# A gated mix of memory attention and a SwiGLU layer on one core: moving value blocks, remainders and two x tables, and ending the seventh Strassen product in the fifth one's bank

## The chip, the core and the metric

The kernel runs on one core of one Trainium2 chip. The metric is the device time of one execution in microseconds (us). Five engines work side by side, each through its own list of instructions in order: PE (TensorE: matmuls; the loads of its weights are the separate row PEld), DVE (VectorE), ACT (ScalarE), POOL (GpSimd) and SP, which here only issues transfers. Matmuls write into eight PSUM banks; a bank is called bank0 to bank7 below.

## The reference

For 2048 rows `x` of width 576, an attention branch `a` and a feed-forward branch `b` are mixed by a gate per row. The attention has 32 heads of width 18 and works in four segments of 512 rows: softmax inside a segment, and a running memory `M`, `z` from the segments before it.

```
for s in range(4):                       # segments of 512 rows
    p = softmax(qs @ ks.T * scale + mask)
    a_dot = p @ vs
    a_mem = (phi(qs) @ M) / (phi(qs) @ z + 1e-6)
    outs.append(g * a_mem + (1 - g) * a_dot)
    M += phi(ks).T @ vs;  z += sum(phi(ks))
a = concat(outs) @ wo
b = (silu(x @ w_gate) * (x @ w_up)) @ w_down      # inner width 4608
out = sigmoid(x . gate_w) * a + (1 - sigmoid(x . gate_w)) * b
```

## The kernel before, in words

**Numbers.** Every fp32 operand is split into a rounded high part, made by ACT, and a low part (the remainder, value minus high part), made by DVE with a `tensor_sub`. A product is then high times high, high times low and low times high: three matmuls instead of one.

**First stage (0 to some 221 us).** Per segment, nine chains of 14 matmuls give q and k (`qk`), eight steps give the values (`v_step`, lines 383 to 404), and from the second segment on each such step is followed by one memory bank (`mem_step`, lines 449 to 469): five or six small matmuls on `Mm` and `phi`, then four DVE operations. A step n takes rows n//2, bank n%2.

**Second stage (to some 1632 us).** Two halves of the rows (`half` 0 and 1), each with 36 tiles of the inner width: 72 *positions*. A position computes gate and up product of one tile, 2x2 in blocks, by a Strassen form with seven products P0 to P6. `seven(t, j)` issues product j: six 128x512 matmuls (line 1018, weights from a tile `wo_`, x from a slot `xo`) and one for the last 64 rows (line 1021). The results chain through PSUM: P0 goes to bank0 (`a`), ACT copies it to bank1 (`xx`), P2 and P4 add to `a`, P3 adds to `xx`. There are two sums on DVE: `y = a + p5` after P2 (line 1087, called the *y add* here) and `p5 = a + p5` after P4 (line 1095, the *p5 add*). After P4, ACT copies `a` into bank1 once more (line 1094), P6 adds to that copy, and DVE multiplies it with the silu (line 1103).

Between products stands a `tick()`, eight in a position, k = 0 to 7, k = 0 behind P0, 1 behind P1, 2 behind the y add, 3 behind P3, 4 behind the p5 add, 5 and 6 behind P5, 7 behind P6. A tick runs `beat`, which first calls what was deferred to it and then adds attention and down products:

- *Deferred work* is the next position's weights: sums of raw tiles on POOL (`total`), high parts on ACT (`high`), remainders on DVE (`low`, line 271). The tables `HIGH` and `LOW` give the tick of each; product 4's remainder comes at k = 1 and product 6's at k = 3 of the position that uses it. The results `hh`, `hl` of a position are split two ticks later in the same way (`split_by`, line 963), the first remainder of them at k = 1.
- *Down products* (`down_group`, line 868): nine matmuls into one of bank3, 4 and 7 and one DVE add into `ya` (line 878). Sixteen of them come in every third position (f % 3 == 0, f > 0), called a *position with groups* here, two or three in a tick from k = 2.
- *Attention steps* (`att_gen`). A unit has six steps; steps 0 to 4 each put a set of logits in a bank (`s_bank`, bf16 matmuls of line 726, row maxima on DVE, line 732); one step later ACT makes the exponentials (`e_bank`, line 744), three steps later DVE rounds them (`p_bank`, line 758) and POOL subtracts (line 759), then a transfer transposes them. A finished unit becomes a *value block* (`v_unit`): 40 small matmuls (lines 774 and 775) and a DVE reduction (line 781). While groups are pending, it is issued at step 5, otherwise at the next unit's step 0, just ahead of that step's logits.

`ts_tile` picks the bank for logits and value blocks: the longest unused of 5 and 6 while groups are pending, else of 5, 6, 7, 3, 4; the first request after groups were fed may get bank7 (`fed`).

At the change of halves ten beats without products (`BREAK`) hold the last sixteen groups. There the second half's x is loaded, summed by POOL and split into new slots (`x_second`, by the tables `LOADS`, `SUMS` and `PARTS`: beat, x half, product). Beat numbers 8 to 17 of these tables lie in the break, 18 to 25 are ticks 0 to 7 of the second half's first position.

When attention has ended, `c_open` frees its memory and loads the output weights `wo` in six pieces into tiles named `raw` (`wo_load`, line 910), which ACT and DVE split five and seven beats later. The **last stage** (from some 1632 us) transposes attention results and multiplies them with `wo`, mixed with the last down products.

Order on each engine is the order in which this program is written out; waits are added where tiles or banks are shared.

Of the kernel before, what the change touches and what calls it, by code (L numbers as in the profile page):

```python
# [20 lines left out]
P = 128  # L21
S = 2048
D = 576
# [25 lines left out]
SHARE = (0, 0, 2, 2, 3, 3, 3, 3)  # L49
BREAK = 10  # L50
LOADS = ((-3, 0, 0), (-2, 0, 1), (3, 1, 0), (4, 1, 3), (4, 0, 3), (5, 0, 2), (5, 1, 1), (6, 1, 2))
SUMS = ((2, 0, 1), (9, 0, 4), (10, 0, 2), (10, 1, 1), (11, 1, 4), (12, 0, 6), (12, 1, 2), (13, 1, 6))
PARTS = ((1, 0, 0), (4, 0, 1), (10, 1, 0), (10, 0, 5), (11, 0, 3), (11, 1, 5), (12, 1, 3), (13, 0, 4), (14, 0, 2),
         (14, 1, 1), (15, 1, 4), (16, 1, 2), (17, 0, 6), (18, 1, 6))
FIRST = (9, 10, 11, 15, 17, 17, 19)
SLOT = (0, 3, 2, 1, 4, 6, 5)
RPOS = (0, 1, 4, 2, 5, 6, 3)
# [9 lines left out]
def gated_mix(ctx, tc, xT, xrest, wf, wfr, wfh, wd, wv, wo, beta, cmask, ident, bmask, out):  # L67
# [39 lines left out]
    first_tile = banks(0, 1, 2, 3, 4)  # L107
    lone_tile = banks(7)
    v_tile = banks(5, 6, 7, 4, 0, 5, 6, 7, *8 * (5, 6, 7))
    a_tile = banks(0)  # L110
    x_tile = banks(1)
    y_tile = banks(2)
    taken = {}
    clock = [0]
# [7 lines left out]

    def ts_tile(shape=(P, L)):
        ids = (5, 6) if groups else (5, 6, 7, 3, 4)
        if fed and groups[0][0] < FT // CH - 1 and max(taken, key=taken.get) != 7:
            ids = (7,)
        fed.clear()
        return ps.tile(list(shape), F32, name=f"bank{soonest(ids, HELD)}")

    def group_tile(shape=(P, L)):  # L130
        return ps.tile(list(shape), F32, name=f"bank{soonest((3, 4, 7), 1)}")

    groups = []

    def split(hi, lo, src):
        nc.scalar.activation(hi, src, AF.Copy)
# [119 lines left out]
    def w_make(half, f, LOW=LOW):  # L256
        g, u = wraw_of.pop(f)
        ops = wops[half, f] = [None] * 7
        a11, a12, a21, a22 = g[:, 0:2], g[:, 2:4], u[:, 0:2], u[:, 2:4]
        src = [a11, None, None, a12, None, None, a22]  # L260

        def total(j, p, q, sub=True):
            src[j] = rp.tile([P, 2, P], F32, name="ws", bufs=3)
            (nc.gpsimd.tensor_sub if sub else nc.gpsimd.tensor_add)(src[j], p(), q())  # L264

        def high(j):
            ops[j] = op_tile()
            nc.scalar.activation(ops[j][:, 0], src[j], AF.Copy)

        def low(j):  # L270
            nc.vector.tensor_sub(ops[j][:, 1], src[j], f32(ops[j][:, 0]))  # L271

        def keep(j):
            nc.sync.dma_start(wc[f, j], f32(ops[j]).rearrange("p a k n -> p (a k n)"))

        todo = [(LEAD - 2, lambda: total(1, lambda: a21, lambda: a22, False)),
                (LEAD - 1, lambda: total(2, lambda: src[1], lambda: a11)),
                (LEAD + 2, lambda: total(4, lambda: a11, lambda: a21)),
                (LEAD + 4, lambda: total(5, lambda: a12, lambda: src[2]))]
        for j in range(7):  # L280
            todo += [(HIGH[j], lambda j=j: high(j)), (LOW[j], lambda j=j: low(j))]
            if half == 0 and f < KEPT:
                todo.append((LEAD + j + 3, lambda j=j: keep(j)))
        return sorted(todo, key=lambda t: t[0])
# [3 lines left out]
    with ExitStack() as st:  # L288
# [310 lines left out]
        for s in range(NSEG):  # L599
# [58 lines left out]
            for n in range(8):  # L658
                hf, i = divmod(n, 4)
                flush()  # L660
                v_step(s, hf, i)
                if s:
                    mem_step(s, n // 2, n % 2)
                if s < 3:
                    if n == 0:
                        xs_of[s + 1] = x_tiles(s + 1)
                    if 1 <= n < 6:
                        x_split(xs_of[s + 1], n - 1, raws["x", n - 1])
                else:
                    if n == 4:  # L670
                        wraw_of[1] = [w_load(1, u) for u in range(2)]
                    if n < 2:
                        first_sum(6, n)
                    elif n < 6:
                        if n < 4:
                            nc.gpsimd.memset(f32(rhs[n - 2][96:]), 0.0)
                        if 3 <= n < 5:
                            r_fetch(n - 3)
                    if n > 2:
                        for z in stack_loads(0)[2 * n - 6:2 * n - 4]:  # L680
                            nc.sync.dma_start(*z)
                    for _ in range((0, 0, 2, 3, 3, 3, 3, 3)[n]):
                        if start[0][0] < 8:
                            start.pop(0)[1]()
# [5 lines left out]
    with ExitStack() as st:  # L690
# [107 lines left out]
        def att_gen():  # L798
# [6 lines left out]
            for tau in range(N + 10):  # L805
# [13 lines left out]
                    e_bank(z)  # L819
                if n == 5 and 1 <= u <= 2 * NB:  # L820
                    held.append(u)
                if held and (groups or n == 0):
                    v = held.pop()
                    v_unit(v - 1)
                    if v % 4 == 1 and v // 4 + 1 < 4 * NSEG:
                        v_fetch(v // 4 + 1)
# [73 lines left out]
        def gates():  # L900
            nc.vector.tensor_scalar_add(gg, gg, 1.0)
            nc.vector.reciprocal(gg, gg)
            nc.vector.tensor_scalar(g1, gg, -1.0, 1.0, op0=OP.mult, op1=OP.add)

        def wo_load(n, hf, c):
            box = []

            def load():
                box.append(raw_tile()[:, :96 * NT].rearrange("p (k n) -> p k n", n=96))
                nc.sync.dma_start(box[0], wo[:, :, 288 * hf + c.start:288 * hf + c.stop])  # L910

            defer(n, load)
            defer(n + 5, lambda: nc.scalar.activation(wos[hf][:, 0, :, c], box[0], AF.Copy))
            defer(n + 7, lambda: nc.vector.tensor_sub(wos[hf][:, 1, :, c], box[0], f32(wos[hf][:, 0, :, c])))
# [45 lines left out]

        def split_by(k, hi, lo, src):
            defer(k, lambda: nc.scalar.activation(hi, src, AF.Copy))  # L962
            defer(k + 1, lambda: nc.vector.tensor_sub(lo, src, f32(hi)))  # L963

        def beat(k=None, half=0):
            for fn in due.popleft() if due else ():
# [62 lines left out]
        for pos, (half, f) in enumerate(seq):  # L1029
# [27 lines left out]
            def tick():  # L1057
# [4 lines left out]
                if half == 0:  # L1062
                    if (q, k) in ((0, 3), (1, 3), (2, 2)):
                        draw[f] = d_load(f)
                    if (q, k) in ((1, 1), (1, 7), (2, 4)):
                        g = f - 1 if k == 1 else f
                        ds[half, g] = d_split(g, draw.pop(g))
                elif (q, k) in ((1, 0), (1, 2), (2, 1)):
                    g = f - 1 if k == 0 else f
                    ds[half, g] = d_fetch(g)  # L1070
                beat(k, half)

            ops, rem = wops.pop((half, f)), rhs[f % 2]
            hh = fp.tile([P, 2, L], F32R, name="hh")
            hl = fp.tile([P, 2, L], F32R, name="hl")
            hs[half, f] = hh, hl
            a, y, xx = a_tile(), y_tile(), x_tile()
            p5, sg0, sg1 = (row_tile() for _ in range(3))
            seven(a, 0)
            nc.scalar.activation(xx, a, AF.Copy)  # L1080
# [4 lines left out]
            seven(a, 2, False)  # L1085
            y = y_tile()
            nc.vector.tensor_add(y, a, p5)
            tick()
            seven(xx, 3, False)
            nc.scalar.activation(sg0, xx, AF.Copy)  # L1090
            tick()
            seven(a, 4, False)
            xx = x_tile()
            nc.scalar.activation(xx, a, AF.Copy)  # L1094
            nc.vector.tensor_add(p5, a, p5)  # L1095
            tick()
            nc.scalar.activation(sg0, sg0, AF.Silu)  # L1097
            seven(y, 5, False)
            nc.scalar.activation(sg1, y, AF.Silu)
            tick()  # L1100
            tick()
            seven(xx, 6, False)
            nc.vector.tensor_mul(sg0, xx, sg0)
            nc.vector.tensor_mul(sg1, p5, sg1)
            if q == CH - 1:
                defer(2, lambda t=(hh[:, 0], hl[:, 0], sg0): split(*t))
# [112 lines left out]
```

## Time and profile before

| what | value |
|---|---|
| median of 3 runs | 1724.15 us (1723.75 to 1724.97) |
| profiled execution: its time, and its span | 1724.43 us, 1722.7 us |
| PE busy | 1706.5 us (99%) |
| weight loads (PEld) busy | 1481.0 us (86%) |
| DVE busy | 1359.8 us (79%) |
| ACT busy | 1084.8 us (63%) |
| POOL busy | 938.4 us (54%) |
| DMA queue q1, share of 16 engines | 77.5% |

The profile is of one execution; times in the timeline are us from the span's start. A row of the timeline has start, length, engine, line, operation, operands, how many were merged, and in brackets the idle time ahead of it with what ended it. Matmuls are pipelined and their ends modelled, so a short stall of PE is counted as busy: the distance between starts tells more than the idle time does.

### The profile page before, as it was taken

What the parts mean: (1) busy time and instruction counts of PE and PEld (TensorE: products, weight loads), DVE (VectorE), ACT (ScalarE), POOL (GpSimd) and SP (SyncE); (2) the same over time, 40 slices, a digit from 0 to 9 for tenths busy, and PEclk for the clock granted to TensorE, in tenths of its full rate; (3) what the DMA queues carried; (4) which work ended last, traced back from release to release, by engine and by line L of the source; (5) the groups of instructions that cost most, each with busy time, mean ns of one, the idle gap of its engine ahead of it and who ended that gap; (6) DMA issues with size and microseconds to landing.
All of it is one profiled execution on the core that took longest, in us unless ns stands there. A gap on an engine that the chain in (4) does not pass through costs nothing.

```text
span 1722.7 us, 34832 instructions
## 1 busy us (share of the span) xinstructions
PE 1706.5 (99%) x11868; PEld 1481.0 (86%) x11868; DVE 1359.8 (79%) x3231; ACT 1084.8 (63%) x2123; POOL 938.4 (54%) x1194
## 2 busy tenths in 40 slices
PE   9999999999999999999999999999999999999999
PEld 7899978888888888888887888888888888888899
DVE  6557588898899889898989677788887778778655
ACT  7666585776677577667765755765666576566411
POOL 4434646666666656565666555555555555555221
PEclk9999999999999999999999999999999999999999
DMA  8654499999998898988879986887778677767544
GB/s 284 233 186 153 151 311 191 232 226 186 209 227 192 181 215 200 193 198 203 210 144 256 290 177 133 178 186 162 148 181 182 147 157 185 163 132 167 165 144 137
DMA packets 524002, 328.05 MB, mean 190 GB/s; under 512 B 411184, under 2 KB 460336, under 8 KB 523824
## 3 DMA queue, kind: packets, MB, share of 16 engines
q1 hardware_dynamic: 523824, 325.83, 77.5%
q8 instruction: 93, 1.52, 0.4%
q14 instruction: 85, 0.70, 0.1%
HBM read 165.76 MB, written 76.09 MB: 140 GB/s over the span
## 4 chain that ended last, share of the span: by engine, by line
PE 83%; DVE 6%; ACT 5%; DMA 3%; issue 2%; POOL 1%; SPq 1%; DVEq 0%; ACTq 0%; POOLq 0%
PE bank L1018 33%; PE bank L868 24%; PE bank L159 10%; PE bank L1021 5%; PE bank L726 4%; PE bank L774 2%; PE bank L775 1%; PE bank L414 1%; ACT pe L744 1%; ACT L744 1%; PE bank L460 1%; DVE xo L137 1%; DVE p L758 1%; DVE scr L732 1%; PE bank L350 1%
## 5 line engine op out<-in xcount | busy, mean ns | idle before, releaser
L759 POOL TENSOR_TENSOR p<-pe,p 128x512 f16<-128x512 f32 x320 | 376.0, 1175 | 420.4 <-DVE p L758 406.2
L868 PE MATMUL bank<-dw,hh 128*128 128x320 f32 (+1 forms) x2304 | 489.0, 305 | 2.8 <-DVE ya L878 2.8
L868 PEld LDWEIGHTS bank<-dw,hh 128*128 128x128 f32 x2304 | 381.4, 190 | 14.4 <-DVE ya L878 3.8
L744 ACT ACTIVATE pe<-bank,mb 128x512 f32<-128x512 f32 (+3 forms) x512 | 247.9, 526 | 197.7 <-DVE mb L732 191.3
L868 PE MATMUL bank<-dw,hl 128*128 128x320 f32 (+1 forms) x1152 | 340.6, 296 | 0.2 <-DVE hl L137 0.2
L732 DVE CUSTOM_DVE_ANT_0 scr<-bank,cm 128x512 bf16<-128x512 f32 (+3 forms) x512 | 246.6, 482 | 6.8 <-PE bank L726 0.2
L878 DVE TENSOR_TENSOR ya<-bank,ya 128x320 f32<-128x320 f32 x352 | 158.3, 453 | 83.9 <-PE bank L868 83.2
L868 PEld LDWEIGHTS bank<-dw,hl 128*128 128x128 f32 x1152 | 218.0, 189 | 0.4 <-DVE hl L137 0.4
L1021 PE MATMUL bank<-xr,rh 128*128 128x512 f32 x504 | 196.5, 390 | 0.0
L752 POOL TENSOR_SCALAR_AFFINE_SELECT pe<-pe 128x256 f32<-128x256 f32 (+1 forms) x320 | 149.8, 469 | 54.1 <-ACT pe L744 51.0
L758 DVE CAST p<-pe 128x512 f16<-128x512 f32 x320 | 152.5, 477 | 0.0
L264 POOL TENSOR_TENSOR ws<-raw 128x256 f32<-128x256 f32 x140 | 118.3, 845 | 17.4 <-DMA raw<-in_wf_dram 4.5
L726 PE MATMUL bank<-kst,qst 108*128 108x512 bf16 (+3 forms) x512 | 125.2, 306 | 2.1 <-ACT pe L744 2.1
L1021 PEld LDWEIGHTS bank<-xr,rh 128*128 128x128 f32 x504 | 94.7, 188 | 20.3
L963 DVE TENSOR_TENSOR hl<-row,hh 128x512 fp32r<-128x512 f32 x120 | 104.2, 868 | 8.3 <-ACT hh L962 7.8
L1095 DVE TENSOR_TENSOR row<-bank,row 128x512 f32<-128x512 f32 x72 | 49.7, 690 | 64.7 <-ACT bank L1094 64.5
L744 ACT ACT_TABLE_LOAD x69 | 88.5, 1283 | 11.1 <-DVE mb L732 10.1
L1080 ACT ACTIVATE bank<-bank 128x512 f32<-128x512 f32 x72 | 41.9, 582 | 80.5 <-PE bank L1021 77.4
L1090 ACT ACTIVATE row<-bank 128x512 f32<-128x512 f32 x72 | 43.3, 601 | 78.0 <-PE bank L1021 77.8
L1097 ACT ACT_TABLE_LOAD x71 | 91.1, 1283 | 1.3
L264 POOL TENSOR_TENSOR ws<-raw,ws 128x256 f32<-128x256 f32 x70 | 58.3, 833 | 49.4 <-DVE wo__22504 L271 10.9
L159 PE MATMUL bank<-xo,qhi 128*128 128x512 f32 x264 | 83.2, 396 | 0.4 <-ACT vps L399 0.4
(2166 smaller groups left out, 4097.9 us busy)
## 6 DMA issues: line engine op xcount, KB each, us to landing
raw<-in_wf_dram SPq DMA_DIRECT2D x140, 256.0 KB
rh<-rc SPq DMA_DIRECT2D x72, 336.0 KB
dc<-dw SPq DMA_DIRECT2D x36, 576.0 KB
dw<-dc SPq DMA_DIRECT2D x36, 576.0 KB
stk<-q SPq DMA_DIRECT2D x32, 384.0 KB
draw<-in_wd_dram SPq DMA_DIRECT2D x36, 288.0 KB
rc<-rt SPq DMA_DIRECT2D x42, 224.0 KB
vd<-vps SPq DMA_DIRECT2D x8, 912.0 KB
```

Of the source, the lines that this page charges most:

```text
L159: nc.tensor.matmul(t, st[n], mv[n], start=(n == 0), stop=(n == 13))
L264: (nc.gpsimd.tensor_sub if sub else nc.gpsimd.tensor_add)(src[j], p(), q())
L726: nc.tensor.matmul(t[:, c:c + w], qs[:KR, pr, P * i:P * i + P], ks[:KR, pr, 0:w], start=True, stop=True)
L732: nc.vector.tensor_tensor_reduce(scr[:, :w], t[:, c:c + w], cm[:, L - w:L], -SCALE, 3.0e38, OP.add, OP.min, m[:, k:k + 1])
L744: nc.scalar.activation(pe[:, c:c + w], t[:, c:c + w], AF.Exp, bias=m[:, k:k + 1], scale=SCALE)
L752: nc.gpsimd.affine_select(d, d, pattern=pat, compare_op=OP.is_ge, fill=0.0, base=0, channel_multiplier=1)
L758: nc.vector.tensor_copy(p[:, 0], pe)
L759: nc.gpsimd.tensor_sub(p[:, 1], pe, p[:, 0])
L868: nc.tensor.matmul(ts[m], p, q[:, cs], start=(n == 0), stop=(n == 3 * CH - 1))
L878: nc.vector.tensor_add(ya[:, i, cs], t, ya[:, i, cs])
L1018: nc.tensor.matmul(t, w[:, p, z], x[z][:, q], start=first and n == 0, stop=False, skip_group_check=True)
L1021: nc.tensor.matmul(t, rem[:, RPOS[j]], XR[j], start=False, stop=True, skip_group_check=True)
```

## The change

Seven edits:

1. **Seventh product.** `a` and `xx` take their banks in turn from 0, 1, 1, 0. P6 adds onto `a` itself, ACT's copy of line 1094 is gone, and the multiplication reads `a`.
2. **Remainders behind the two sums.** In ticks 1 and 3 the remainders made by `low` and `split_by` are put aside (`behind`) and issued after the y add or the p5 add (`let_go`).
3. **Values with logits.** A value block is always issued at step 0, ahead of that step's logits; only logits use up the mark `fed`.
4. **Memory banks in pairs.** In the first stage both memory banks of a row tile follow the odd step.
5. **x's parts.** `SUMS` and `PARTS` get other beats: four parts of the first x half move to beats 17 to 22, most of the second half's come a beat or two earlier.
6. **Output weights.** Pieces 3 and 4 are loaded into new tiles `wr`, the fifth into the tile `draw`, instead of `raw`.
7. Nothing else is computed or left out; sums and products are the same.

```diff
-SUMS = ((2, 0, 1), (9, 0, 4), (10, 0, 2), (10, 1, 1), (11, 1, 4), (12, 0, 6), (12, 1, 2), (13, 1, 6))
-PARTS = ((1, 0, 0), (4, 0, 1), (10, 1, 0), (10, 0, 5), (11, 0, 3), (11, 1, 5), (12, 1, 3), (13, 0, 4), (14, 0, 2),
-         (14, 1, 1), (15, 1, 4), (16, 1, 2), (17, 0, 6), (18, 1, 6))
+SUMS = ((2, 0, 1), (9, 0, 4), (10, 1, 1), (11, 1, 4), (12, 1, 2), (13, 1, 6), (14, 0, 2), (19, 0, 6))
+PARTS = ((1, 0, 0), (4, 0, 1), (10, 1, 0), (11, 1, 5), (12, 1, 3), (13, 0, 5), (13, 1, 1), (14, 1, 4), (15, 1, 2),
+         (17, 0, 2), (17, 1, 6), (18, 0, 3), (20, 0, 4), (22, 0, 6))
...
-    a_tile = banks(0)
-    x_tile = banks(1)
+    ax_tile = banks(0, 1, 1, 0)
...
-        if fed and groups[0][0] < FT // CH - 1 and max(taken, key=taken.get) != 7:
-            ids = (7,)
-        fed.clear()
+        if fed and len(shape) == 2:
+            if groups[0][0] < FT // CH - 1 and max(taken, key=taken.get) != 7:
+                ids = (7,)
+            fed.clear()
...
+    stash, holds = [], [False]
+
+    def behind(fn):
+        if holds[0]:
+            stash.append(fn)
+        else:
+            fn()
+
+    def let_go():
+        while stash:
+            stash.pop(0)()
...
         def low(j):
-            nc.vector.tensor_sub(ops[j][:, 1], src[j], f32(ops[j][:, 0]))
+            behind(lambda: nc.vector.tensor_sub(ops[j][:, 1], src[j], f32(ops[j][:, 0])))
...
-                if s:
-                    mem_step(s, n // 2, n % 2)
+                if s and n % 2:
+                    for bank in range(2):
+                        mem_step(s, n // 2, bank)
...
-                if held and (groups or n == 0):
+                if held and n == 0:
...
+        def wo_home(n):
+            if n in (4, 5):
+                return cps[0].tile([P, 96 * NT], F32, name="wr", bufs=2)
+            if n == 8:
+                return fp.tile([P, D], F32, name="draw", bufs=1)[:, :96 * NT]
+            return raw_tile()[:, :96 * NT]
...
-                box.append(raw_tile()[:, :96 * NT].rearrange("p (k n) -> p k n", n=96))
+                box.append(wo_home(n).rearrange("p (k n) -> p k n", n=96))
...
-            defer(k + 1, lambda: nc.vector.tensor_sub(lo, src, f32(hi)))
+            defer(k + 1, lambda: behind(lambda: nc.vector.tensor_sub(lo, src, f32(hi))))
...
+                holds[0] = k in (1, 3)
                 beat(k, half)
+                holds[0] = False
...
-            a, y, xx = a_tile(), y_tile(), x_tile()
+            a, y, xx = ax_tile(), y_tile(), ax_tile()
...
             nc.vector.tensor_add(y, a, p5)
+            let_go()
             tick()
...
             seven(a, 4, False)
-            xx = x_tile()
-            nc.scalar.activation(xx, a, AF.Copy)
             nc.vector.tensor_add(p5, a, p5)
+            let_go()
             tick()
...
-            seven(xx, 6, False)
-            nc.vector.tensor_mul(sg0, xx, sg0)
+            seven(a, 6, False)
+            nc.vector.tensor_mul(sg0, a, sg0)
```

Two places show what moved. In the changed kernel's rows the same code has other line numbers: 786 and 738 for value blocks and logits, 880 for down products, 1037 for products, 282 and 982 for remainders, 1108 and 1115 for the two sums.

The first is on PE, in position 9 (the first half's tile 9, with groups), from P0 on. Of each run of matmuls into one bank the first row stands here; the bank is the number after `bank`. Before:

```order
L774 MATMUL bank7_4889<-v_3341,pt_4439 128x57
...
L726 MATMUL bank5_4931<-kst1_2324,qst1_2323 128x512
...
L868 MATMUL bank4_4988<-dw_4585,hh_3999 128x320 x2
...
L726 MATMUL bank5_5010<-kst1_2324,qst1_2323 128x128
...
L868 MATMUL bank4_5136<-dw_4585,hh_3999 128x320 x2
...
L774 MATMUL bank6_5154<-v_3341,pt_4771 128x57
...
L1018 MATMUL bank2_4974<-xo60_1736,wo__4880 128x512 x3
...
L726 MATMUL bank5_5228<-kst0_2322,qst0_2321 128x512
```

And after the change:

```order
L786 MATMUL bank5_4871<-v_3360,pt_4425 128x57
...
L738 MATMUL bank7_4913<-kst1_2324,qst1_2323 128x512
...
L880 MATMUL bank4_4970<-dw_4571,hh_3987 128x320 x2
...
L738 MATMUL bank5_4992<-kst1_2324,qst1_2323 128x128
...
L1037 MATMUL bank2_4955<-xo60_1726,wo__4862 128x512 x3
...
L786 MATMUL bank6_5165<-v_3360,pt_4753 128x57
...
L738 MATMUL bank5_5208<-kst0_2322,qst0_2321 128x512
```

The first value block and its logits have changed banks, so that the third set of logits now takes the value block's bank and not that of the first set. The second value block, which stood alone between a down product and P5, now stands right ahead of logits. Counted over the whole list, a value block stands right ahead of logits 62 times of 64 instead of 25 times.

The second place is on DVE, in position 19, from the tick behind P1 to the p5 add. Before:

```order
L271 TENSOR_TENSOR wo__8088<-ws_7941,wo__8088 128x256
L963 TENSOR_TENSOR hl_7602<-row_7607,hh_7601 128x512
L758 CAST p_8186<-pe_8104 128x512
L781 TENSOR_REDUCE acc_8230<-bank3_8189 128x152
L732 ISA scr_8236,mb0_2325<-bank5_8234,cm_84 128x512
L732 ISA mb0_2325 128x1
L1087 TENSOR_TENSOR bank2_8247<-bank0_8150,row_8153 128x512
L271 TENSOR_TENSOR wo__8165<-ws_8083,wo__8165 128x256
L963 TENSOR_TENSOR hl_7602<-row_7608,hh_7601 128x512
L963 TENSOR_TENSOR dw_8176<-draw_7773,dw_8176 128x576
L271 TENSOR_TENSOR wo__8178<-raw_7579,wo__8178 128x256
```

After, in the same stretch:

```order
L770 CAST p_8146<-pe_8066 128x512
L793 TENSOR_REDUCE acc_8190<-bank3_8149 128x152
L744 ISA scr_8196,mb0_2325<-bank5_8194,cm_84 128x512
L744 ISA mb0_2325 128x1
L1108 TENSOR_TENSOR bank2_8207<-bank1_8112,row_8115 128x512
L282 TENSOR_TENSOR wo__8050<-ws_7861,wo__8050 128x256
L982 TENSOR_TENSOR hl_7566<-row_7571,hh_7565 128x512
L282 TENSOR_TENSOR wo__8127<-ws_8045,wo__8127 128x256
L982 TENSOR_TENSOR hl_7566<-row_7572,hh_7565 128x512
L982 TENSOR_TENSOR dw_8138<-draw_7737,dw_8138 128x576
L770 CAST p_8237<-pe_8104 128x512
```

The first two rows of before (product 4's remainder and a remainder of the position before) now stand behind the y add; the last row of before (product 6's remainder) has gone behind the p5 add.

## The prediction

> **What bounds the kernel now.** I read the page first, then PE's waits, then the busy time in stretches, then the timeline where a wait or an edit lies. From the page:
>
> ```profile
> span 1722.7 us, 34832 instructions
> PE 1706.5 (99%) x11868; PEld 1481.0 (86%) x11868; DVE 1359.8 (79%) x3231; ACT 1084.8 (63%) x2123; POOL 938.4 (54%) x1194
> ```
>
> PE is the bound: only 16.2 us of the span are not booked as busy. So an edit pays only where it shortens PE's own list or ends one of PE's waits, and ACT's relief alone pays nothing. The waits on PE and on its weight loads, with us in total, times, longest:
>
> ```profile
> PE bank L1018 <- ACT bank L1094: 3.6, 6, 1.4
> PE bank L868 <- DVE ya L878: 2.8, 4, 0.9
> PE bank L726 <- ACT pe L744: 2.1, 6, 0.4
> PE bank L1018 <- DVE bank L1087: 1.1, 2, 0.7
> PEld bank L1018 <- ACT bank L1094: 8.0, 11, 1.9
> PEld bank L1018 <- DVE bank L1087: 3.5, 7, 1.1
> ```
>
> The first and fifth are P6 waiting for ACT's copy, the second is down products in the break, the third logits waiting for exponentials, the fourth and sixth P4 waiting for the y add. The idle times are too small, since modelled ends hide part of each stall:
>
> ```profile
> 616.72 0.39 PE L1021 MATMUL bank<-xr,rh 128*128 128x512 f32 x1
> 617.45 1.66 PE L1018 MATMUL bank<-xo,wo__8378 128*128 128x512 f32 x6 [0.34 <-ACT bank L1094]
> 618.94 0.39 PE L1021 MATMUL bank<-xr,rh 128*128 128x512 f32 x1
> 620.53 0.39 PE L1021 MATMUL bank<-xr,rh 128*128 128x512 f32 x1
> ```
>
> Product to product without a stall is 620.53 - 618.94 = 1.59, so one matmul takes 1.59/7 = 0.227. From 616.72 the next came 0.73 later instead of 0.227 (0.50 lost where 0.34 is shown, 0.16 more), and the six after it took 1.49 instead of 1.36 (0.13 more). Which engine is next to PE, by stretch of 100 us in the first and the second half (columns: PE, PEld, DVE, ACT, POOL busy, clock, DMA, GB/s):
>
> ```profile
> 400.00:500.00 100.00, 99.27 (x691) 84.45 (x689) 90.05 (x212) 69.46 (x136) 63.74 (x87) 1.00 0.95 213
> 1300.00:1400.00 100.00, 100.00 (x717) 85.56 (x717) 79.51 (x198) 64.49 (x128) 56.94 (x72) 1.00 0.79 176
> ```
>
> DVE has 10% to spare in the first half and 20% in the second. What the change asks of DVE at a given moment therefore matters more in the first half.
>
> **The change part by part.**
>
> *Values with logits.* A value block alone, logits alone, and both together, each between two last matmuls of products:
>
> ```profile
> 596.91 0.39 PE L1021 MATMUL bank<-xr,rh 128*128 128x512 f32 x1
> 598.19 0.38 PE L726 MATMUL bank<-kst,qst 108*128 108x512 bf16 x1
> 599.79 0.39 PE L1021 MATMUL bank<-xr,rh 128*128 128x512 f32 x1
> ...
> 601.38 0.39 PE L1021 MATMUL bank<-xr,rh 128*128 128x512 f32 x1
> 601.61 0.39 PE L726 MATMUL bank<-kst,qst 108*128 108x512 bf16 x1
> 603.22 0.39 PE L1021 MATMUL bank<-xr,rh 128*128 128x512 f32 x1
> ...
> 620.76 0.20 PE L774 MATMUL bank<-v,pt 128*128 128x57 bf16 x1
> 623.28 0.39 PE L1021 MATMUL bank<-xr,rh 128*128 128x512 f32 x1
> ```
>
> Both together (596.91 to 599.79, the value block from 597.14 on): 2.88 - 1.59 = 1.29. Logits alone: 1.84 - 1.59 = 0.25. The block alone (620.53 to 623.28): 2.75 - 1.59 = 1.16. Joining saves 1.16 + 0.25 - 1.29 = 0.12. By the order 62 blocks stand ahead of logits instead of 25: 37 x 0.115 = -4.2 us, all on PE's path. What could take it back is that the block's bank is wanted sooner: with groups pending the second logits after it take its bank. Between stand one set of logits and one or two down products, and DVE's reduction (0.62 us) needs its turn in that time; I count nothing, and the range holds it.
> The Trainium skill (TensorE: Matmul & The Clock Gate, section on 56 ns) gives a warm matmul a fixed cost of some 2.5 ns beyond its columns and no price for a neighbour of another kind; by it joining would save nothing and the sum would be 4.2 higher. The rows above differ from it, and no row here shows what the 0.12 is.
>
> *Exponentials.* In positions that open with a value block in bank7 (9, 12, 15 and the like) the third logits waited for the first ones' exponentials:
>
> ```profile
> 385.66 0.38 PE L726 MATMUL bank<-kst,qst 108*128 108x128 bf16 x2 [0.35 <-ACT pe L744]
> ```
>
> They now take the bank of the value block, whose reduction comes ahead of that row maximum on DVE. Six waits of 0.35 + 0.16 = -3.1. For the wait on that reduction nothing is counted.
>
> *Memory banks in pairs.* After a memory bank the next step's matmuls come late:
>
> ```profile
> 96.92 0.82 PE L460 MATMUL bank<-Mm,ph 128*128 128x114 f32 x6
> 97.54 1.86 PE L159 MATMUL bank<-vw,xo 128*128 128x290 f32 x12
> 99.23 0.43 PE L159 MATMUL bank<-vw,xs 128*128 128x290 f32 x2
> 99.50 0.68 PE L460 MATMUL bank<-Mm,ph 128*128 128x152 f32 x4
> ```
>
> Two matmuls take 99.50 - 99.23 = 0.27; the twelve before took 1.69 instead of 12 x 0.135 = 1.62. So 0.07 a bank, 24 banks in three segments, 12 changes of kind fewer: -0.9. DVE gets eight short operations at once instead of four twice; their banks are wanted two steps later.
>
> *x's parts, in the break.* DVE is the engine waited for there:
>
> ```profile
> 930.53 1.77 DVE L137 TENSOR_TENSOR xo<-wo__12935,xo 128x512 fp32r<-128x512 f32 x1
> 942.32 0.56 PE L868 MATMUL bank<-dw,hh 128*128 128x320 f32 x2 [0.94 <-DVE ya L878]
> ```
>
> By `PARTS`, ten remainders of x stood in beats 10 to 16 and seven stand there now; counted in the order, two fewer lie ahead of the add that the last group waits for. The stalls are 2.8 + 4 x 0.16 = 3.4 us; two remainders of 0.7 to 1.77 cover 1.4 to 3.4 of it. I take -2.0. The three parts now in ticks 0, 2 and 4 have a product between them and their use (P3, P4, P6), 1.59 against an operation on each of ACT and DVE; a late one costs some tenths.
>
> *The seventh product.* ACT's copies go:
>
> ```profile
> L1094 ACT ACTIVATE bank<-bank 128x512 f32<-128x512 f32 x72 | 42.2, 587 | 64.4 <-PE bank L1021 64.0
> 1626.69 0.61 ACT L913 ACTIVATE wo<-raw 128x480 fp32r<-128x480 f32 x1 [2.50 <-DMA raw<-in_wo_dram]
> ```
>
> The 42.2 us on ACT pay nothing of themselves. P6's eleven waits go: 3.6 + 6 x (0.16 + 0.13) for the long ones, some 0.2 for each of the other five: -6.3. The longest (1.4) is in the last position, where ACT was held 2.50 us by a piece of `wo` that waited on SP's queue for a free tile; the new tiles end that, so it goes too. But P6 now waits for DVE's p5 add, on which nothing hung so soon before. This is the disputed term.
>
> *Remainders behind the sums.* The y add is no longer queued behind two remainders. P4's waits (by starts 1.1 + 2 x 0.29 and some 0.2 for each of five) are 2.7; I take -2.2. The price is at the p5 add. Position 19, which has no groups, on DVE:
>
> ```profile
> 595.41 1.38 DVE L271 TENSOR_TENSOR wo__8088<-ws,wo__8088 128x256 fp32r<-128x256 f32 x1
> 597.21 1.10 DVE L963 TENSOR_TENSOR hl<-row,hh 128x512 fp32r<-128x512 f32 x1 [0.41 <-ACT hh L962]
> 598.23 0.41 DVE L758 CAST p<-pe 128x512 f16<-128x512 f32 x1
> ...
> 600.28 0.70 DVE L1087 TENSOR_TENSOR bank<-bank,row 128x512 f32<-128x512 f32 x1 [0.50 <-PE bank L1021]
> 600.89 0.41 DVE L271 TENSOR_TENSOR wo__8165<-ws,wo__8165 128x256 fp32r<-128x256 f32 x1
> 601.23 0.68 DVE L963 TENSOR_TENSOR hl<-row,hh 128x512 fp32r<-128x512 f32 x1
> 601.83 0.75 DVE L963 TENSOR_TENSOR dw<-draw,dw 128x576 fp32r<-128x576 f32 x1
> ...
> 604.32 0.69 DVE L1095 TENSOR_TENSOR row<-bank,row 128x512 f32<-128x512 f32 x1 [0.46 <-ACT bank L1094]
> ```
>
> Before, DVE did both remainders (595.41, 597.21) while PE ran, and still stood 0.50 ahead of the y add. Now it stands longer, and does them after it. It was free for the p5 add at 604.32 - 0.46 = 603.86. Product 6's remainder (0.34 from start to start, as at 600.89) leaves; the two enter with 0.34 + 0.60 if unslowed (600.89 to 601.83) or about 1.30 + 1.02 as they ran. The add starts at 604.46 or 605.84 and ends 0.69 later, at 605.15 or 606.53. P6 could start at 604.81 + 0.227 = 605.04, P4's end (603.22 + 0.39) being long past. So this position loses 0.1 to 1.5 where it lost nothing. On the page L963's mean is 868 ns against 0.68 here, and I give each remainder 0.2: 0.1 + 0.4 = 0.5. The first half has 24 positions without groups: 24 x 0.5 = 12. With groups, nine down products stand between P4 and P6 and cover it. In the second half DVE's doubled spare time does; I count nothing there.
>
> *The sum*, against the profiled execution, 1724.43 (span 1722.7 and 1.7 around it, 0.3 above the median): -4.2 - 3.1 - 0.9 - 2.0 - 6.3 - 2.2 = -18.7, and +12: -6.7, 1717.7; on the median's scale **1717.4 us**.
>
> **The rivals.**
>
> *Slower: DVE's list sets the pace.* Each sum blocks DVE, and the time in front of the y add is lost in all 24 positions, at 1.0 (between 0.5 and the 1.5 of position 19's rows): 1724.1 - 18.7 + 24 = 1729.4. For it: 90% busy, and two blocking points in 12 us. Against it: a late P6 itself gives DVE time, and the next position with groups lets it catch up. It turns slower than before from 18.7/24 = 0.78 a position. Chance 0.16.
> The Trainium skill (PSUM — Partial Sum Buffer, section on engine and sequencer instructions) calls VectorE's queue strict FIFO, which speaks against this edit; the 0.50 at 600.28, with work behind it, agrees.
>
> *Faster: DVE keeps up.* The remainders run unslowed, at 0.1: 24 x 0.1 = 2.4, 1724.1 - 18.7 + 2.4 = 1707.8. For it: the rows from 600.89 to 602 ran unslowed, and the p5 add no longer waits out ACT's copy. Against it: remainders slowed threefold (1.38) in the same list. Chance 0.27.
>
> *Joining is worth nothing*, as PE's list would be as long with the small matmuls elsewhere: 1717.4 + 4.2 = 1721.6. Against it are the three pairs of rows above. Chance 0.06.
>
> **How the numbers follow.** The forecast has 0.51; its own range, 0.35 to 0.75 a position, is 1713.8 to 1723.4. The range for 8 in 10 reaches into both sides: 1706 (2 us beyond the faster rival) to 1730. About 0.2% (3.4 us) is what a measurement of this kernel tells from no change: faster is below 1720.7, same up to 1727.6. Faster: 0.27 + 0.51 x 0.7 = 0.63. Same: 0.51 x 0.3 + 0.06 = 0.21. Slower: 0.16.
>
> **What would show it right or wrong.** In the changed profile the waits of line 1018 on ACT's copy are gone, and a row of line 1018's successor waiting for the p5 add stands in their place, mostly in the first half; no logits wait for exponentials at the openings of positions 9, 12 and 15; a value block between products costs 1.29 together with its logits; the break's waits for `ya` are under 2 us. The forecast is wrong if the p5 add's row is under 4 us (then 1708) or over 19 us (then slower), or if a wait of logits for the value block's reduction appears.

## The result and the profile after

The changed kernel takes **1742.45 us** (median, 1740.78 to 1743.02) against 1724.41 for the kernel before in the same runs: a ratio of 1.0098, 95% interval 1.0086 to 1.0111. It is 18 us slower where 7 us faster were forecast. The profiled execution took 1742.59 (span 1740.9), the one before 1724.43.

The head of the page, and four of the waits on PE (us in total, times, longest):

```profile
span 1740.9 us, 34814 instructions
PE 1713.3 (98%) x11868; PEld 1477.3 (85%) x11868; DVE 1355.7 (78%) x3231; ACT 1048.3 (60%) x2051; POOL 933.3 (54%) x1194
```

```profile
PE bank L1037 <- DVE row L1115: 13.0, 21, 2.5
PE bank L880 <- DVE hl L148: 1.8, 2, 1.6
PE bank L880 <- DVE ya L890: 1.4, 5, 0.5
PE bank L738 <- ACT pe L756: 0.5, 1, 0.5
```

Line 1037 is the product's matmul (1018 before), line 1115 the p5 add (1095). The waits for ACT's copy are gone, the logits' for exponentials went from 2.1 us to 0.5, those of the down products for `ya` from 2.8 to 1.4, and P4's 1.1 for the y add are gone. In their place stands one row that is longer than all of these were (3.6 + 2.8 + 2.1 + 1.1 = 9.6): P6 waiting for the p5 add. One more wait belongs to it: the view puts 1.35 us at 441.76 down to ACT (line 981), but that is a P6 too, and it starts right behind the p5 add, which ends at 441.62. The second row shown, 1.6 of it in the last position, comes up again below. DVE has no more to do: it was busy for 1359.8 us and is so for 1355.7. It waits more, and at one place. The two sums in the view of DVE's groups (busy time, mean ns of one, and the idle time just ahead of it with what ended that), first before, then after:

```profile
L1087 DVE TENSOR_TENSOR bank<-bank,row 128x512 f32<-128x512 f32 x72 | 50.1, 696 | 26.0 <-PE bank L1021 12.5 <-ACT row L1083 11.4 <-ACT hh L962 1.9
L1095 DVE TENSOR_TENSOR row<-bank,row 128x512 f32<-128x512 f32 x72 | 49.7, 690 | 64.7 <-ACT bank L1094 64.5
```

```profile
L1108 DVE TENSOR_TENSOR bank<-bank,row 128x512 f32<-128x512 f32 x72 | 50.3, 699 | 79.8 <-PE bank L1040 39.9 <-ACT row L1104 30.1 <-ACT hh L981 9.2
L1115 DVE TENSOR_TENSOR row<-bank,row 128x512 f32<-128x512 f32 x72 | 49.4, 686 | 24.0 <-PE bank L1040 24.0
```

Ahead of the y add DVE stood idle for 26.0 us and stands so for 79.8; all but 2.3 of that in the 50 positions without groups, where it was 0.52 us a position and is 1.55. How that becomes a stall is seen in position 14, which has no groups. DVE before, where two remainders still run ahead of the y add:

```profile
490.50 0.80 DVE L271 TENSOR_TENSOR wo__6534<-ws,wo__6534 128x256 fp32r<-128x256 f32 x1
491.22 0.68 DVE L963 TENSOR_TENSOR hl<-row,hh 128x512 fp32r<-128x512 f32 x1
492.41 0.70 DVE L1087 TENSOR_TENSOR bank<-bank,row 128x512 f32<-128x512 f32 x1 [0.52 <-ACT row L1083]
```

The same place after, DVE and then PE:

```profile
498.26 0.70 DVE L1108 TENSOR_TENSOR bank<-bank,row 128x512 f32<-128x512 f32 x1 [1.80 <-ACT row L1104]
498.87 0.42 DVE L282 TENSOR_TENSOR wo__6506<-ws,wo__6506 128x256 fp32r<-128x256 f32 x1
499.20 0.69 DVE L982 TENSOR_TENSOR hl<-row,hh 128x512 fp32r<-128x512 f32 x1
499.81 0.96 DVE L282 TENSOR_TENSOR wo__6526<-ws,wo__6526 128x256 fp32r<-128x256 f32 x1
500.69 0.68 DVE L982 TENSOR_TENSOR hl<-row,hh 128x512 fp32r<-128x512 f32 x1
...
502.44 0.69 DVE L1115 TENSOR_TENSOR row<-bank,row 128x512 f32<-128x512 f32 x1
```

```profile
502.17 0.39 PE L1040 MATMUL bank<-xr,rh 128*128 128x512 f32 x1
503.27 1.63 PE L1037 MATMUL bank<-xo,wo__6554 128*128 128x512 f32 x6 [0.71 <-DVE row L1115]
```

DVE stands 1.80 us instead of 0.52, then does the two held remainders (498.87, 499.20) and the rest of its list, and comes to the p5 add at 502.44 without having waited for it: the operands were there, DVE was late. The add ends at 503.13. P6 was due at 502.17 + 0.227 = 502.40 and starts at 503.27, 0.87 late.

Counted by starts, as the prediction counted (each matmul's distance to the next, less the usual one), what product 6's matmuls lose went from 6.3 to 25.3 us: in the first half 18.9 us over the 25 positions without groups (22 of them lose over 0.15), in the second 6.3 (11 of 25). All matmuls of products took 21.1 us longer, memory banks 1.4; down products took 2.7 less and logits 2.3 less; the rest adds 0.6. The sum is 18.1.

### The profile page after: what moved, and what is told of

It reads as the page before. It is cut to its first block, busy times and chain, and to the rows that moved or that the text cites. A ratio compares the mean times of both kernels' runs of the same rounds, so it can differ in the third digit from the quotient of the medians.

```text
span 1740.9 us, 34814 instructions
## 1 busy us (share of the span) xinstructions
PE 1713.3 (98%) x11868; PEld 1477.3 (85%) x11868; DVE 1355.7 (78%) x3231; ACT 1048.3 (60%) x2051; POOL 933.3 (54%) x1194
## 5 line engine op out<-in xcount | busy, mean ns | idle before, releaser
L764 POOL TENSOR_SCALAR_AFFINE_SELECT pe<-pe 128x256 f32<-128x256 f32 (+1 forms) x320 | 145.0, 454 | 60.8 <-ACT pe L756 52.9
L770 DVE CAST p<-pe 128x512 f16<-128x512 f32 x320 | 158.0, 495 | 0.0
L275 POOL TENSOR_TENSOR ws<-raw 128x256 f32<-128x256 f32 x140 | 113.9, 814 | 15.0 <-DMA raw<-in_wf_dram 8.6
L1108 DVE TENSOR_TENSOR bank<-bank,row 128x512 f32<-128x512 f32 x72 | 50.3, 699 | 79.8 <-PE bank L1040 39.9
L982 DVE TENSOR_TENSOR hl<-row,hh 128x512 fp32r<-128x512 f32 x120 | 96.3, 803 | 0.0
L275 POOL TENSOR_TENSOR ws<-ws,raw 128x256 f32<-128x256 f32 x70 | 70.5, 1008 | 45.9 <-POOL ws L275 5.9
```

The lines of the kernel that those rows point to most:

```text
L764: nc.gpsimd.affine_select(d, d, pattern=pat, compare_op=OP.is_ge, fill=0.0, base=0, channel_multiplier=1)
L770: nc.vector.tensor_copy(p[:, 0], pe)
```

## Experiments

The theories on record. **A**: the held remainders, let go between the two sums, make the p5 add late. **B**: taking ACT's copy away is the cost, whatever the order on DVE. **C**: the held remainders are late for the products that read them. From these came **D**: DVE idles ahead of the y add with the held work behind it, and all of its list runs late; against **E**: tick 3's hold is the harm, by product 6's own remainder. In the table "idle" is DVE's idle time ahead of the y add, from the view of groups; the medians of before in the four sets of runs were 1724.98, 1725.84, 1725.23 and 1725.04. The profiled execution of a_no_hold took 1725.26, 3.5 us above its median; its trace has a stretch at half the clock (last section). Those of the others lie within 2 us of theirs.

| kernel | held at ticks | ACT's copy | other edits | us | ratio, 95% interval | idle, us |
|---|---|---|---|---|---|---|
| before | none | yes | none | 1725 | 1 | 26.0 |
| the change | 1 and 3 | no | all | 1742.45 | 1.0086 to 1.0111 | 79.8 |
| a_no_hold | none | no | all | 1721.73 | 0.9974 to 0.9993 | 26.6 |
| a_act_copy | 1 and 3 | yes | all | 1748.71 | 1.0120 to 1.0154 | 76.1 |
| a_neither | none | yes | all | 1720.83 | 0.9967 to 0.9986 | 24.8 |
| b_join | none | yes | joined blocks only | 1719.02 | 0.9954 to 0.9980 | 27.2 |
| hold_tick1 | 1 | no | all | 1755.07 | 1.0158 to 1.0189 | 78.3 |
| hold_tick3 | 3 | no | all | 1718.16 | 0.9944 to 0.9972 | 25.5 |
| neither_single | none | yes | all but the pairs | 1718.04 | 0.9944 to 0.9973 | 26.0 |
| copy_p6_free | 1 and 3, not P6's | yes | all | 1735.56 | 1.0043 to 1.0073 | 73.9 |
| best | 3 | no | all but the pairs | 1717.68 | 0.9939 to 0.9966 | 27.2 |
| best_copy | 3 | yes | all but the pairs | 1729.21 | 1.0015 to 1.0036 | 25.3 |
| b_tick1 | 1 | yes | none | 1739.22 | 1.0066 to 1.0093 | 74.6 |
| tick1_weight | 1 (weights), 3 | no | all | 1724.03 | 0.9987 to 1.0007 | 37.6 |

### Each of the two edits on the products undone

a_no_hold:

```diff
-                holds[0] = k in (1, 3)
+                holds[0] = False
```

> The changed kernel with the remainders no longer held back: each is issued in its own tick again, so the y add and the p5 add stand behind them on DVE as before. Product 6 still reads the bank of product 4 and so waits for the p5 add. Theory A (the held remainders, let go between the two sums, make the p5 add late): product 6's waits fall from 25 us to about 7, product 4's rise by 1 to 2: 1724 to 1727 us. Theory B (taking ACT's copy away is the cost, since product 6 now waits for DVE's list whatever its order): product 6 keeps 15 us or more, 1735 us or above.

a_act_copy:

```diff
-    ax_tile = banks(0, 1, 1, 0)
+    a_tile = banks(0)
+    x_tile = banks(1)
...
             seven(a, 4, False)
+            xx = x_tile()
+            nc.scalar.activation(xx, a, AF.Copy)
             nc.vector.tensor_add(p5, a, p5)
...
-            seven(a, 6, False)
-            nc.vector.tensor_mul(sg0, a, sg0)
+            seven(xx, 6, False)
+            nc.vector.tensor_mul(sg0, xx, sg0)
```

> The changed kernel with ACT's copy of product 4 back and the banks of before for it; the remainders still held behind the two sums. Product 6 waits for ACT's copy again, not for DVE. Theories A and B both: product 6's waits fall from 25 us to about 6, 1722 to 1725 us. Theory C (held remainders are late for the products that read them, so the hold costs without the bank too): waits of products 0, 4 and 6 for remainders stay at 4 us or more and the time is 1726 or above.

a_neither has both edits.

> The changed kernel with both undone: ACT's copy back and no remainder held; the joined value blocks, the memory banks in pairs, x's later parts and the pieces' new homes stay. By the two traces the joined blocks are worth 8.4 us (waits for exponentials included), the break 2.1, the last position 1.6, the pairs -0.5: 1712 to 1716 us. Theory B or C alone makes no other forecast here; if the time is above 1720, the loss of the changed kernel is not all in these two edits.

Measured: 1721.73, 1748.71 and 1720.83. Without the hold 21 us come back, and DVE's idle time ahead of the y add is 26.6 again, as before the change:

```profile
L1108 DVE TENSOR_TENSOR bank<-bank,row 128x512 f32<-128x512 f32 x72 | 50.1, 695 | 26.6 <-ACT row L1104 12.3 <-PE bank L1040 12.1 <-ACT hh L981 1.9
```

So B falls: without a hold it makes no clear difference (0.9 us, inside both intervals) whether P6 waits for ACT's copy or for the p5 add. A had the direction for a_no_hold, but not the size: 1721.73 is below its 1724 to 1727, and in the profiled execution product 6 still loses 11.9 us by starts, not 7. For a_act_copy A and B both forecast 1722 to 1725, and it came out the slowest of the three; C, that the hold costs by itself, is what its waits show. In position 11 of a_act_copy P6 waits twice, for the copy and then, at its third matmul, for its own weight remainder:

```profile
444.44 0.73 PE L1038 MATMUL bank<-xo,wo__5666 128*128 128x512 f32 x2 [1.31 <-ACT bank L1117]
445.50 1.19 PE L1038 MATMUL bank<-xo,wo__5666 128*128 128x512 f32 x4 [0.32 <-DVE wo__5666 L283]
```

Of a product's six matmuls the third is the first to read the weight's remainder. By starts it loses 16 us there, in 31 positions.

a_neither, with all that is not one of these two edits, was expected at 1712 to 1716 and took 1720.8. What was missing was looked for in the next two.

### The joined blocks alone

b_join changes the kernel before in one place, besides the rule of the bank that goes with it:

```diff
-                if held and (groups or n == 0):
+                if held and n == 0:
```

> The kernel before with one edit: value blocks always stand with the logits and take the bank by the new rule. If a block of small matmuls costs 0.12 us at its edge (my two terms of 4.2 and 3.1): 7 to 9 us faster, 1715 to 1717 us. If joining is worth nothing and only the exponentials' waits go: 3 us faster, 1721 us.

Measured: 1719.02, 6.0 us faster; below the 7 to 9 expected and well above the 3 of the waits alone. By the interval the gain is 3.5 to 7.9 us. So the change of kind at a block's edge has its price, as the prediction read from three pairs of rows. By starts, all blocks of small matmuls with their edges went from 152.6 us (359 blocks) to 145.3 (322); in the changed kernel they are at 144.2.

### Memory banks

neither_single is a_neither with one more edit undone, a memory bank at every step:

```diff
-                if s and n % 2:
-                    for bank in range(2):
-                        mem_step(s, n // 2, bank)
+                if s:
+                    mem_step(s, n // 2, n % 2)
```

> The changed kernel without the hold, with ACT's copy back (1720.8 us so far), and with one more edit undone: a memory bank at every step again, not two at every other. In the trace of that kernel the pairs put eight short operations at the segment's end on DVE where four stood, and positions 0 and 1 are 2.2 us behind the kernel that has the joined blocks alone, with a wait of product 2 that the other has not. Theory: the pairs cost 2 to 4 us there: 1717 to 1719 us, product 2's wait of 0.9 gone. Rival (the pairs are worth nothing either way, by the rows of their matmuls): 1720 to 1722 us.

Measured: 1718.04, 2.8 us faster than with the pairs. The two intervals overlap a little (0.9967 to 0.9986 with the pairs, 0.9944 to 0.9973 without), so it is the rows that carry this. The pairs cost part of what a_neither missed, and the rows say why nothing was gained for it. Two single banks in the kernel before, then a pair in the changed one:

```profile
99.50 0.83 PE L460 MATMUL bank<-Mm,ph 128*128 128x152 f32 x6
100.16 1.85 PE L159 MATMUL bank<-vw,xo 128*128 128x290 f32 x12
```

```profile
100.92 1.56 PE L471 MATMUL bank<-Mm,ph 128*128 128x152 f32 x12
102.28 0.91 PE L170 MATMUL bank<-vw,xo 128*128 128x290 f32 x5
```

The single banks hold PE for 100.16 - 99.50 = 0.66 and, by the row at 96.92, 0.62; together 1.28. The pair holds it for 102.28 - 100.92 = 1.36: the 0.08 is paid between the two banks of a pair as it was behind a single one. The price came on DVE, where a pair's eight short operations stand ahead of other work. In a_neither the first y add comes at 227.76, behind the last pair's eight and behind product 2, where b_join has it at 225.92. Product 2 has waited:

```profile
225.77 1.66 PE L1038 MATMUL bank<-xo,wo__2473 128*128 128x512 f32 x6 [0.77 <-ACT bank L1102]
```

This wait is for ACT's copy of P0 (line 1102), which comes at 225.15 in a_neither and at 223.38 in neither_single. Ahead of it on ACT stand copies of values that wait for DVE's add of line 406 (1.84 and 0.60 us), and the first of these adds comes at 222.03, behind the eight operations of the pair before (219.56 to 221.79). neither_single has no such wait of product 2.

### Which hold

hold_tick1 and hold_tick3 are the changed kernel with `k == 1` and with `k == 3` in place of `k in (1, 3)`.

> The changed kernel with only tick 1's remainders held (those behind the y add); tick 3's are issued in place. With no hold it took 1721.7 us, with both 1742.5. In the changed kernel DVE stood 33 us ahead of the y add in the first half, without the hold 8. Theory D (DVE stands idle ahead of the y add with the held remainders behind it, so its list runs late and P6 waits for the p5 add): most of the loss stays, 1736 to 1743 us, DVE idle ahead of the y add 25 us or more in the first half. Theory E (tick 3's hold is the harm, since product 6's own remainder comes after the p5 add): 1721 to 1726 us.

> The changed kernel with only tick 3's remainders held (those behind the p5 add); tick 1's are issued in place. Theory D: little of the loss, 1720 to 1726 us; the p5 add comes earlier than without any hold, and product 6's waits for it fall from 10 us to 5 or less in the first half, with some waits of product 6 for its own remainder in their place. Theory E: 1735 us or above, product 6's third matmul waiting for a remainder in 20 positions or more.

Measured: 1755.07 and 1718.16. Tick 1's hold alone costs 33 us over no hold, more than D said (1736 to 1743); tick 3's alone gains 3.6, where D had 1720 to 1726. D has the directions, and its ranges are missed on both sides. P6's wait in the two:

```profile
PE bank L1037 <- DVE row L1115: 29.4, 34, 2.2
```

```profile
PE bank L1037 <- DVE row L1115: 1.3, 2, 1.1
```

E falls. With tick 1's hold the two remainders of tick 1 enter between the sums; tick 3's hold takes work out from there, which is why both together (1742) are better than tick 1's alone.

copy_p6_free is a_act_copy with product 6's own remainder taken out of the hold:

```diff
-            behind(lambda: nc.vector.tensor_sub(ops[j][:, 1], src[j], f32(ops[j][:, 0])))
+            (behind if j != 6 else lambda fn: fn())(lambda: nc.vector.tensor_sub(ops[j][:, 1], src[j], f32(ops[j][:, 0])))
```

> The changed kernel with ACT's copy back (1748.7 us so far, where product 6's third matmul waits 16 us in 31 positions for a weight remainder), and product 6's own weight remainder taken out of the hold; all other remainders stay held. If the hold costs because this one remainder is let go after the p5 add: 1726 to 1732 us, those waits gone. If DVE's whole list runs late: the waits turn up at other rows, 1736 us or above.

Measured: 1735.56, between the two forecasts. The waits for P6's remainder fall from 16 us to 2.6, 13 us come back, and the other 15 stay. DVE's idle time is still 73.9, and other rows are late: product 0's third matmul now loses 5.8 us in 14 positions to its remainder. So the one late remainder is a place where DVE's lateness shows, and with it gone half of the loss stays.

### Tick 1's hold alone, and with ACT's copy

b_tick1 adds `behind` and `let_go` to the kernel before, for tick 1 and the y add only.

> The kernel before with one edit: the remainders of tick 1 are held until the y add is issued. ACT's copy stays, no block is joined. Theory D (the idle time of DVE ahead of the y add is the cost, whatever else the change does): 1745 to 1760 us, with DVE idle ahead of the y add for 25 us or more in the first half where it was 8. If the hold only costs together with the other edits: 1724 to 1730 us.

Measured: 1739.22, 14.0 us slower. The idle time is as D said; the price is below what it said:

```profile
L1100 DVE TENSOR_TENSOR bank<-bank,row 128x512 f32<-128x512 f32 x72 | 50.2, 697 | 74.6 <-PE bank L1032 38.7 <-ACT row L1096 28.1 <-ACT hh L973 7.6
L1109 DVE TENSOR_TENSOR row<-bank,row 128x512 f32<-128x512 f32 x72 | 49.5, 687 | 39.1 <-ACT bank L1108 38.6
```

With the copy, DVE's idle time ahead of the p5 add falls from 64.7 to 39.1: that slack takes up 25.6 of the 48.6 us added ahead of the y add, and no product waits for the p5 add. The 14 us show elsewhere: by starts product 0's matmuls lose 7.3 us more than before, mostly from the third on, the first to read the weight's remainder, and product 6's lose 6.2 more. So the hold needs no other edit to cost, and without the copy it costs more.

best and best_copy have tick 3's hold only and single memory banks, without and with ACT's copy.

> The changed kernel with two things altered: only tick 3's remainders are held (1718.2 us so far), and a memory bank stands at every step again (worth 2.8 us beside the other edits). If the two add up: 1714.5 to 1716.5 us. If the pairs' cost was already taken up by the earlier p5 add: 1717 to 1718.5 us.

> The same with ACT's copy back, so product 6 no longer waits for the p5 add. Without any hold the copy made no difference (1720.8 with it, 1721.7 without). Theory F (the gain of tick 3's hold is the earlier p5 add, which only a product 6 without the copy waits for): no better than the 1718.0 us of the kernel with copy and without hold, 1717.5 to 1721 us. Theory G (tick 3's hold helps of itself): equal to the kernel without the copy, 1714.5 to 1716.5 us.

Measured: 1717.68 and 1729.21. best came out by the second of its forecasts (1717 to 1718.5): the two gains don't add up. It stands level with hold_tick3 and neither_single, their intervals overlap. best_copy is beyond both forecasts: F named the right condition, and the copy makes tick 3's hold a loss, since the p5 add then waits for ACT's copy, and product 6's remainder behind it comes late (its third matmul loses 7.4 us by starts, 0.3 in neither_single):

```profile
L1117 DVE TENSOR_TENSOR row<-bank,row 128x512 f32<-128x512 f32 x72 | 49.8, 692 | 84.6 <-ACT bank L1116 84.6
```

The rule is the same at the second sum: DVE idles 84.6 us there with ready work behind (38.2 in best).

### How much per us of idle time

tick1_weight is the changed kernel, but at tick 1 only product 4's weight remainder is held.

> The changed kernel, where at tick 1 only product 4's own weight remainder is held until the y add is issued; the remainder of hh is issued in its own place again, and tick 3's are all held as in the change. In the changed kernel the two kinds held at tick 1 took 38.3 us (70 weight remainders) and 34.7 us (48 of hh). With neither held there it took 1718.2 us, with both 1742.5. Theory D in its simple form (the price goes with the time of the work that is moved behind the waiting add): about half, 1728 to 1733 us, DVE idle ahead of the y add some 50 us where it was 25.5 and 79.8. Rival (any wait ahead of held work costs the whole, or only the longer remainder of hh does): above 1738, or below 1723 us.

Measured: 1724.03, idle 37.6. Half of the held time was expected to cost half; it costs 5.9 of 24.3 us, a quarter. The idle time explains it: 37.6 - 25.5 = 12.1 us are added where the full hold adds 79.8 - 25.5 = 54.3. The cost of an added us of idle time is 5.9/12.1 = 0.49 here and 24.3/54.3 = 0.45 with the full hold. So the price goes with the idle time that the hold makes, not with the work that it moves. Why one remainder makes a quarter of the idle time was not tried.

These are means of two unlike halves. Between hold_tick3 and the change, which differ in tick 1's hold alone, the first half (from the start of position 0 to that of position 36) takes 16.8 us longer for 25.8 us of added idle time, and the second (to the last matmul of the last P6) 7.2 for 28.5: 0.65 and 0.25 for an added us. tick1_weight gives the same picture, 5.2 for 6.9 and 1.2 for 5.2. In the change DVE is busy for 606.6 of the 715 us from 221 to 936, 85%, and for 552.3 of the 704 from there to 1640, 78%: an idle us cost more in the half where DVE had less to spare. No run alters that spare time alone.

## Why the prediction was wrong

- **Joined blocks and exponentials** (-4.2 and -3.1): right in kind. By starts they gave -8.4 in the changed kernel, by b_join -6.0. The Trainium skill (TensorE: Matmul & The Clock Gate, section on 56 ns) has no price for a change of kind; by it only the waits would have gone, 1725.0 - 3.1 = 1721.9, and 1719.02 was measured.
- **Memory banks in pairs** (-0.9): wrong, +2.8 by neither_single. The edge is paid inside the pair too, and the eight operations that I named and priced at nothing delay DVE at the start of the second stage.
- **x's parts in the break** (-2.0): right there. The break's stalls went from 4.8 to 2.7 us by starts. neither_single, which has this edit, enters the second half 2.6 us ahead of b_join, which hasn't, and keeps 1.5 of it behind the first position, where the parts that moved are made: the "some tenths" of the text were 1.1.
- **P6's old waits** (-6.3): they went, but the 1.6 us of the last position came back at the next wait, where the last down products wait for the remainder `hl`. Right behind it PE ran 3.4 us at half the clock, some 1.7 us more (last section):

```profile
1652.11 0.41 PE L880 MATMUL bank<-dw,hl 128*128 128x320 f32 x1 [1.58 <-DVE hl L148]
```

- **P4's waits on the y add** (-2.2): 1.1 was gained.
- **The new waits of P6** (+12): this is the step that failed. By starts they are 25.3 us instead of 12: 18.9 in the first half, where 24 x 0.5 was forecast (there are 25 such positions, 0.76 each), and 6.3 in the second, where nothing was. The estimate took one position, let the two remainders enter there with 0.5 beyond their usual time, and added nothing for DVE's longer standing ahead of the y add, which the text itself named ("now it stands longer"). That standing grew by 1.03 a position over the 50 without groups, 0.96 in the first half and 1.10 in the second. The sign that was named for it, the p5 add's row over 19 us, did not show: that row has 13.0, since the idle times of PE hide part of each stall. DVE had 10% to spare in the first half, but part of that was time in which it stood ahead of the sums (26.0 and 64.7 us over both halves, the latter for ACT's copy). Over both halves the change added 53.8 us ahead of the first sum and took away 40.7 ahead of the second.
- **The second half**, where DVE's "doubled spare time" was to cover the remainders: it does so in 14 of 25 positions and not in 11. From position 36 to 71 the changed kernel loses 4.2 us on before, and hold_tick3 gains 3.0.
- **Side effects not in the sum**: products 0 and 2 lose 2.5 us more than before by starts. Product 0's are mostly waits for its weight remainders, product 2's is the wait that came with the pairs.

The rival "DVE's list sets the pace" was the mechanism. It had a chance of 0.16 and 1.0 a position in the first half, for 1729.4; the measured time lies 13 us beyond it, and beyond the range. Against the rival I had put that a position with groups lets DVE catch up. It does, as the idle time of 2.3 us there says, and the two positions behind it lose the time again. The rival's own sum was too low as it kept 18.7 of gains: the pairs, P4 and the last position gave 3.7, 1.1 and some 1.6 us less than that, and the half clock behind the last position took 1.7.

## What to carry to other kernels

An engine that takes its work in order loses whatever stands ahead of a wait: before moving ready work behind an operation, read how long that operation waits, and ask whether the work had filled that wait. Moving work from ahead of a waited-for operation to behind it pays only where the engine would have come too late to that operation; here tick 3's move did so (1721.7 to 1718.2), tick 1's cost 33 us (1721.7 to 1755.1), and the same tick 3 move lost 11 us where a copy stood ahead of the sum (1718.0 to 1729.2). Two edits that each are worth nothing or less can only be priced together when one changes what the other waits for.

## What the runs showed of the hardware

Between two memory banks, of 128x152 and then 128x114 columns, PE lost 0.08 us, about what it loses between a memory bank and the 128x290 matmuls that follow it (0.07), so that pairing banks saved nothing. No run tells whether that is for the change of shape or of bank.

An added idle us on DVE ahead of the y add, with DVE 78% busy over the span, cost the kernel 0.45 to 0.49 us without the copy (0.65 in the first half, 0.25 in the second) and 14.0/48.6 = 0.29 with it, although PE bounds the kernel at 98% busy.

A wait of PE can cost more than its length. In the change's trace PE waits 1.58 us until 1652.11, and from 1652.90 to 1656.30 the granted clock is 0.50: a 128x288 matmul takes 0.24 us from start to start there (1653.23 to 1653.47) and 0.13 after it (1660.48 to 1660.61). Half of 3.4 us is 1.7, 0.1% of the span, and the mean granted clock is 0.999 in all four executions of the change. a_no_hold's trace has one such stretch, at 248.4 behind a wait of 2.28 us; hold_tick1's has two, at 247.4 and 445.4, at waits of 2.18 and 1.89. No stretch follows the wait of 2.47 us at 247.39 in the change, so the length of the wait alone does not decide it, and no run shows what does.
